# A fused RWKV6 attention and expert block: other order of work in the first steps, in step six, and of one weight addition

## The chip, the core and the metric

The kernel runs on one core of one Trainium2 chip. Such a core has five engines, each with its own queue of instructions that runs in order: TensorE (PE in the profile, its weight loads PEld), VectorE (DVE), ScalarE (ACT), GpSimd (POOL) and SyncE (SP), which here only issues transfers. ScalarE issues some transfers too. The metric is the time of one execution on the device in microseconds (us); lower is better. The kernel before takes 573.67 us, the median of three runs from 573.4 to 574.68.

## The reference

```python
def _attn_ref(r, k, v, w, u):                 # batch 4, heads 8, seq 768, head_dim 48
    state = np.zeros((B, H, D, D)); y = np.zeros_like(r)
    for t in range(S):
        kt, vt, rt, wt = (k[:, :, t], v[:, :, t], r[:, :, t], w[:, :, t])
        cur = np.einsum('bhd,bhe->bhde', u[None] * kt, vt)
        y[:, :, t] = np.einsum('bhd,bhde->bhe', rt, state + cur)
        state = wt[:, :, :, None] * state + np.einsum('bhd,bhe->bhde', kt, vt)
    return y

def _moe_ref(x, w_in, w_out):                 # 3072 tokens, d_model 384, d_ff 2048
    h = x @ w_in
    sp = np.maximum(h, 0.0) + np.log1p(np.exp(-np.abs(h)))
    return (h * erf(sp)) @ w_out              # x is y with the heads side by side
```

The first part is a recurrence over time, with a decay w that differs for each channel and time; u is a bonus for the token itself. The second is a two-layer block over all tokens with the activation h * erf(softplus(h)). The weights w_in and w_out are given in float64 and have to be made into float32 on the chip.

## The kernel before, in words

**Steps.** The work is cut into 12 steps (s = 0 to 11): six stretches of 128 tokens for each of two halves of the batch. In a step each 128 tokens are two chunks of 64 (HC). Inside a chunk the recurrence is done by levels: at level n, pairs of neighbouring blocks of 2^(n-1) tokens meet, r of the right block with k of the left block. `level_products` (line 691) is the matmul of one level into a PSUM bank `pp`; `scale` (lines 357 in step zero and 364 elsewhere) is VectorE's product that multiplies the halves of r and k in place by the decay over the level's blocks; `take_level` (lines 701, VectorE with a mask, and 708, ScalarE, for level 6) puts the products in their place in the matrix `own`. The next level's matmuls need the scale, and the scale overwrites what this level's matmuls read. The decays over blocks, the totals, are made by GpSimd (`plan_totals`, line 386, for steps 0 and 1; `prepare`, line 438, for the others). For level 1 a copy `rk1` is made, in which one half is multiplied by u (`multiply_u`, lines 408 to 419).

Then `from_own` (line 723) multiplies `own` with v into the PSUM tile `y`, `state_part` (line 798) makes the new part of the state from v and the transposed k (`kT`), `middle` is the state between the two chunks, `through_state` (line 749) adds what comes from the state to `y`. ScalarE copies `y` into `xT`; a part of it, `y3`, goes to other rows, by transfers (line 784), or in step zero by a matmul, the `hop` (line 764). `fence` (line 732) is a small VectorE copy that reads `y`.

**The second block.** `hidden` (line 1206) is x @ w_in for a step, eight pieces of 12 passes, each emptied by ScalarE (line 1215). `project` (line 1238) is the second matmul for step 0, and `project_fast` (line 1328) for the later ones, a scheme with seven products instead of eight which needs sums of weights (`mix_weights`, line 1266) and of the gated values (`blend`, lines 1305 to 1311). They are put between the parts of later steps' attention.

**The weights.** `convert` turns 16 blocks (0 to 7 of w_in, 8 to 15 of w_out) into float32. For each block there is a load by SP ("l", lines 271 to 275, let go by a one-element copy that waits for something on purpose), two ScalarE operations ("b", line 289 or 291, and "r", line 297), one or two of VectorE ("h", lines 306 and 311) and an add on GpSimd ("o", line 319). "j" is "h" and "o" together. The strings of CONVERT say which of them are sent at which level of steps 1 to 3.

**The order.** It is written out by hand: the program is under a manual schedule, so each engine runs its instructions in the order in which Python issues them. A generator made by `prepare` for the next step (`following`) is advanced by `next(following)` at chosen places. Step 0 is `attend_first`, steps 1 to 4 `attend`, steps 5 to 11 `attend_late`. In the last, strings such as "s P" say what is put where: s is a softplus on ScalarE, P a piece of `project_fast`, H one of `hidden`, F a turn of `following`. DIRECT is 4; steps 7 to 11 are "joined", steps 5 and 6 are not.

**The start.** `load_first` issues SP's loads of r, k, u, w and the masks; `stay_warm` (line 1034) issues matmuls on the identity that nothing reads, six before the first useful products and two twice among the level-1 products of step 0; `keep_busy` (line 1043) issues a matmul on zeros into a bank that is not yet used. `wait_for` (line 942) is a one-element GpSimd copy that waits for a scale.

## Time and profile before

| | before |
|---|---|
| median of three runs | 573.67 us (573.4 to 574.68) |
| the profiled execution | 573.88 us, span 572.1 us |
| PE busy | 563.8 us, 99% of the span |
| VectorE busy | 452.4 us, 79% |
| ScalarE busy | 359.2 us, 63% |
| GpSimd busy | 244.6 us, 43% |
| transfers | 63.24 MB, mean 111 GB/s |

A row of the timeline has the start in us from the beginning of the span, the duration, the engine, the line of the kernel, the operation, the tile that is written and what is read, and in brackets how long the engine was idle before it and what ended that. Matmuls in float32 appear as two passes each, so "x12" is six matmuls. The ends of matmuls are modelled, so PE looks busy across short gaps; the starts show them. A row of the chain of waits has start, duration, engine, tile and line.

### The profile page before, as it was taken

How to read it: one execution, taken by the hardware profiler on the slowest of the kernel's cores; microseconds unless marked ns; L12 is line 12 of the kernel's file. 1: busy time of each engine (PE TensorE's matmuls, PEld its weight loads, DVE VectorE, ACT ScalarE, POOL GpSimd, SP SyncE). 2: the span in 40 equal slices, each digit the busy share in tenths (PEclk: the TensorE clock that was granted, in tenths of full speed). 3: DMA queues.
4: the chain of work that ended last, by engine and by line, in shares of the span. 5: the costliest groups of instructions: out<-in, count | busy, mean ns of one | idle time of the engine just before them, and what ended most of it. 6: DMA issues, size and time to landing. Idle time of an engine off the chain costs nothing.

```text
span 572.1 us, 16713 instructions
## 1 busy us (share of the span) xinstructions
PE 563.8 (99%) x7320; PEld 501.2 (88%) x7320; DVE 452.4 (79%) x509; ACT 359.2 (63%) x495; POOL 244.6 (43%) x262
## 2 busy tenths in 40 slices
PE   8999999999999999999999999999999999999997
PEld 6688887578998998998998898899899899989997
DVE  7776886999899999699789689689778587477730
ACT  3658877646368867756765766666775771489500
POOL 3567380832884884283575176077073000000000
DMA  8596671440426215245235236335232301000000
GB/s 264 192 315 252 218 230 58 172 158 10 148 69 183 82 63 181 42 147 173 41 123 199 39 111 203 48 112 166 47 111 85 47 9 35 3 2 1 28 29 28
DMA packets 54081, 63.24 MB, mean 111 GB/s; under 512 B 35160, under 2 KB 40568, under 8 KB 52984
## 3 DMA queue, kind: packets, MB, share of 16 engines
q1 hardware_dynamic: 53624, 61.98, 34.4%
q8 instruction: 57, 0.93, 0.7%
q10 hardware_dynamic: 384, 0.20, 0.1%
q14 instruction: 16, 0.13, 0.1%
HBM read 52.39 MB, written 8.69 MB: 107 GB/s over the span
## 4 chain that ended last, share of the span: by engine, by line
PE 75%; DVE 5%; POOL 2%; ACT 1%; issue 1%; ACTq 0%; POOLq 0%
PE m L1328 33%; PE m L1206 27%; PE c L1431 6%; PE pp L691 2%; PE y L723 2%; PE y L749 1%; DVE in L364 1%; PE pp L798 1%; POOL tot_sb L438 1%; POOL w_out_sb L319 1%; PE m L1238 1%; DVE h L1171 1%; PE c L1328 0%; ACTq L784 0%; PE pp L1116 0%
## 5 line engine op out<-in xcount | busy, mean ns | idle before, releaser
L1206 PE MATMUL m<-xT,w_in_sb 128*128 128x256 f32 x960 | 214.5, 381 | 0.2 <-ACT h L1215 0.2
L1206 PEld LDWEIGHTS m<-xT,w_in_sb 128*128 128x128 f32 x960 | 180.1, 190 | 25.2 <-ACT h L1215 0.6
L364 DVE TENSOR_TENSOR in<-in,tot_sb 128x1024 f32<-128x1024 f32 (+1 forms) x55 | 75.7, 1375 | 6.3 <-PE pp L691 5.0
L1215 ACT COPY h<-m 128x512 f32<-128x512 f32 x80 | 46.2, 580 | 51.6 <-PE m L1206 51.3
L1328 PE MATMUL m<-mixed,h 128*128 128x192 f32 x320 | 56.7, 331 | 0.0
L1328 PE MATMUL m<-w_out_sb,h 128*128 128x192 f32 x320 | 56.1, 329 | 0.0
L1328 PEld LDWEIGHTS m<-mixed,h 128*128 128x128 f32 x320 | 51.8, 190 | 0.8
L1328 PEld LDWEIGHTS m<-w_out_sb,h 128*128 128x128 f32 x320 | 52.0, 190 | 0.5
L1328 PE MATMUL m<-w_out_sb,room 128*128 128x192 f32 x288 | 49.7, 326 | 0.0
L1328 PEld LDWEIGHTS m<-w_out_sb,room 128*128 128x128 f32 x288 | 47.3, 190 | 0.1
L493 POOL TENSOR_TENSOR words<-words,own 128x384 f32<-128x384 f32 x21 | 31.2, 1488 | 26.4 <-DVE words L524 13.0
L1166 ACT ACT_TABLE_LOAD x28 | 35.9, 1283 | 8.7 <-DVE h L1171 6.7
L691 PEld LDWEIGHTS pp<-in 48*48 48x48 f32 (+4 forms) x2368 | 30.1, 120 | 11.2 <-issue 5.4
L534 POOL TENSOR_TENSOR words<-words 128x384 f32<-128x384 f32 x28 | 38.7, 1410 | 0.0
L486 POOL TENSOR_TENSOR own<-rest 128x384 f32<-128x384 f32 x7 | 8.5, 1210 | 69.2 <-ACT o L1334 69.2
L1162 ACT ACT_TABLE_LOAD x28 | 35.9, 1283 | 1.8 <-issue 1.3
L691 PE MATMUL pp<-in 48*48 48x32 f32 (+4 forms) x2368 | 33.9, 206 | 0.6 <-DVE in L364 0.6
L438 POOL TENSOR_TENSOR tot_sb<-tot_sb 128x256 f32<-128x256 f32 (+4 forms) x50 | 30.8, 616 | 3.8
L559 DVE TENSOR_REDUCE sums<-rk 128x16 f32<-128x768 f32 (+2 forms) x31 | 31.3, 1022 | 0.0
L1162 ACT ACTIVATE room<-h 128x1024 f32<-128x1024 f32 x28 | 29.6, 1057 | 0.3
L534 POOL TENSOR_TENSOR rk<-words 128x384 f32<-128x384 f32 x28 | 29.6, 1088 | 0.0
L319 POOL TENSOR_TENSOR w_out_sb<-w_out_sb,rest 128x768 int32<-128x768 int32 x8 | 18.7, 2340 | 21.6 <-DVE w_out_sb L311 21.6
(215 smaller groups left out, 1013.2 us busy)
## 6 DMA issues: line engine op xcount, KB each, us to landing
in<-in_rkw SPq DMA_DIRECT2D x8, 1024.0 KB, 5.2
words<-in_moe_w_in SPq DMA_DIRECT2D x16, 384.0 KB, 5.4
words<-in_moe_w_out SPq DMA_DIRECT2D x16, 384.0 KB, 5.9
words<-in_rk_rows SPq DMA_DIRECT2D x8, 768.0 KB, 5.4
w<-in_rkw SPq DMA_DIRECT2D x11, 512.0 KB, 6.8
v<-in_v SPq DMA_DIRECT2D x12, 384.0 KB, 5.7
out<-o SPq DMA_DIRECT2D x23, 192.0 KB, 3.6
in<-in_rkw SPq DMA_DIRECT2D x7, 512.0 KB, 5.8
```

Of the source, the lines that this page charges most:

```text
L364: nc.vector.tensor_mul(halves, halves, view(tots[level - 1], 0, [[1, n], [2, nb], [0, half]]))
L438: nc.gpsimd.tensor_mul(new, pair[:, :, 0], pair[:, :, 1])
L493: engine.tensor_mul(to, to, of[:, :, None, :].to_broadcast([P, NEAR // 2 // half, half, D]))
L534: engine.tensor_mul(to[:, i], r[:, half:], k[:, part * rows + i, None].to_broadcast([P, half, D]),)
L559: nc.vector.tensor_reduce(out=to, in_=of, axis=mybir.AxisListType.X, op=ALU.add)
L691: nc.tensor.matmul(to, lhsT=rk(1, n)[rows(e), s0 : s0 + m], rhs=right, start=True, stop=True,)
L1162: nc.scalar.activation(sp_room, chunks[0], AF.Softplus)
L1166: nc.scalar.activation(at, sp_room, AF.Erf)
L1206: nc.tensor.matmul(ps[:, ff, :], lhsT=w_in_sb[:, g * FG + f + ff, kk * P : (kk + 1) * P], rhs=xT[:, kk, :], start=kk == 0, stop=kk == KT - 1,)
L1215: nc.scalar.copy(h[:, f : f + FT, :], ps[:])
L1328: nc.tensor.matmul(to, lhsT=a[:, f], rhs=b[:, f], start=start and f == 0, stop=f == FG - 1, skip_group_check=True,)
L1431: nc.tensor.matmul(to[:, f], lhsT=turns["weights"][b][:, i * FT + f], rhs=turns["tokens"][a], start=a + b in STARTS and not f, stop=True, ...
```

## The change

It has these parts, and nothing else of the program differs.

- The load of u is issued by ScalarE, ahead of its first table load, and no longer by SP between the first two loads of r and k.
- Seven warming products are issued at the start, not six.
- In step 0, level 5 (MASKED) is put in its place by four ScalarE copies of 16 rows (`take_blocks`), not by VectorE's masked copy.
- The copy `rk1` of step 1: the half for r stays on ScalarE at the same place; the half for k is made by GpSimd (two products and a copy) behind step 0's last `wait_for`.
- The load of weight block 1 is let go by the total of level 5 on GpSimd, at level 4, and no longer by `own` at level 2; the load of w for step 1 stays behind it on SP. The load of block 2 is let go by a ScalarE copy behind `middle`, not by a GpSimd copy behind `fence`.
- The eight transposes of k in step 0 go to one bank, without the `keep_busy` before them; VectorE copies the first half, ScalarE the second. One of the two conversions "h" of block 0 comes ahead of `fence`. "b" of block 1 and its "r" and "h" come behind `through_state`.
- In step 1, "h" of a block comes behind `scale` at every level, and at level 1 behind the product that writes `own`.
- In step 3, the first turn of `following` is left out at level 2 and made up at level 3. With this the addition "o" of the weight block that is sent at level 3 is issued ahead of step 4's totals on GpSimd and no longer behind them.
- In step 6 alone, the first project piece P comes behind `from_own`, `through_state` and the load of the next step.

```diff
@@ -193,8 +193,8 @@
         turns["first"] = t5 = t[:].rearrange("p x n t -> p (x n t)").rearrange(
             "p (j x n t) -> p j x n t", j=NJ, x=2, n=NP
         )
+        nc.scalar.dma_start(out=u_sb[:], in_=u)
         nc.sync.dma_start(out=t5[:, 0], in_=rkw[0][:, 0:2, b0])
-        nc.sync.dma_start(out=u_sb[:], in_=u)
         nc.sync.dma_start(out=t5[:, 1, 0], in_=rkw[0][:, 0, b1])
         nc.sync.dma_start(out=t5[:, 1, 1], in_=rkw[0][:, 1, b1])
         nc.sync.dma_start(out=ws[0][:, b0], in_=rkw[0][:, 2, b0])
@@ -411,6 +411,15 @@
                     )
                     nc.vector.tensor_copy(out=plain[0], in_=plain[1])
                     return
+                if s == 1 and x:
+                    for j in range(NJ):
+                        of = slice(j * NP, (j + 1) * NP)
+                        nc.gpsimd.tensor_mul(
+                            with_u[0][:, of], with_u[1][:, of],
+                            u_sb[:, :, None].to_broadcast([P, NP, C // 2]),
+                        )
+                    nc.gpsimd.tensor_copy(out=plain[0], in_=plain[1])
+                    return
                 for p in range(NP):
                     of = slice(p, None, NP)
                     nc.scalar.mul(
@@ -422,6 +431,7 @@
                 for i in range(parts):
                     for x in range(2):
                         multiply_u(i, x)
+                        yield
                 return
             yield
             yield
@@ -711,6 +721,18 @@
 
 
 
+    def take_blocks(own, pp, level):
+
+        half = 1 << (level - 1)
+        got = pp[:].rearrange("p e n t -> p (e n) t")
+        for s0 in range(0, C, HC):
+            for b in range(HC // 2 // half):
+                of = slice(s0 + 2 * b * half, s0 + (2 * b + 1) * half)
+                t = (2 * b + 1) * half
+                nc.scalar.copy(
+                    own[of, :, t : t + half], got[of, :, b * half : (b + 1) * half]
+                )
+
     def from_own(s, own, swap):
         vt = loaded[s][1]
         for j in range(NJ):
@@ -872,12 +894,15 @@
         level_products(pp, RK, LOG - 1)
         scale(s, LOG - 1)
         take_level(own, pp, LOG - 1)
-        run("front", None)
+        behind = before and not joined
+        run_late(s, "s" if behind else "s P")
         if before:
             from_own(before, ready[before][0], 0)
             through_state(before, xTs[before])
             if s + 1 < n_steps:
                 load_step(s + 1)
+        if behind:
+            run_late(s, "P")
         if joined:
             ps = state_products()
             next(following, None)
@@ -956,7 +981,7 @@
                 scale(0, level, batch=j)
             turns["pp"] = products([P, NE, JP, HC])
             keep_busy(turns["pp"], (DM,))
-            take_level(own, pp, level)
+            (take_blocks if level == MASKED else take_level)(own, pp, level)
             wait_for(1 << level - 1)
             if level == 2:
                 totals(2, part=slice(batch // 2, batch))
@@ -966,10 +991,11 @@
                 stages["b"](0, 0)
                 stages["b"](0, 1)
                 stages["r"](0)
-                for _ in prepare(1):
-                    pass
+                second = prepare(1)
+                next(second)
                 nc.sync.dma_start(out=vt[:], in_=v[0])
-                stages["l"](1, own[:, 0, 2:3])
+            if level == LOG - 2:
+                stages["l"](1, ready[0][1][LOG - 1][:, 0:1])
                 nc.sync.dma_start(out=ws[1][:], in_=rkw[1][:, 2])
         totals = plan_totals(1)
         pp = turns.pop("pp")
@@ -977,46 +1003,42 @@
             level_products(pp, first_pair, LOG, half)
             scale(0, LOG, batch=j)
         take_level(own, pp, LOG)
+        wait_for(HC - 1)
+        next(second)
 
         kT = att.tile([P, NH, D], FP32, name="kT", bufs=1)
         kT_by_e = kT[:].rearrange("p (e n) d -> p e n d", e=NE)
-        turned = [products([P, NE, JP, HC])]
-        keep_busy(turned[0], (DM,))
-        for j, half in enumerate(halves):
-            if j:
-                turned.append(products([P, NE, JP, HC]))
-            for i, n in enumerate(half):
-                nc.tensor.transpose(
-                    turned[j][:, 0, 2 * i : 2 * i + 2], first_pair(1, n), ident[:]
-                )
+        turned = products([P, JP, P])
+        turns["next"] = 1 - turns["next"]
+        for n in range(JP):
+            nc.tensor.transpose(turned[:, n, :], first_pair(1, n), ident[:])
         from_own(0, own, 1)
-        for half, ps, copy in zip(halves, turned, (nc.scalar.copy, nc.vector.tensor_copy)):
+        for half, copy in zip(halves, (nc.vector.tensor_copy, nc.scalar.copy)):
             copy(
                 kT_by_e[:, :, half.start : half.stop],
-                ps[:, 0].rearrange("p (n e) d -> p e n d", e=NE)[..., :D],
+                turned[:, half.start : half.stop].rearrange("p n (e d) -> p e n d", e=NE)[..., :D],
             )
-        stages["b"](1, 0)
-        stages["b"](1, 1)
+        stages["h"](0)
         fence()
-        stages["l"](2, seen[:, 0:1])
-        load_v(1)
-        stages["h"](0)
         stages["h"](0)
         ps = [[products([P, NE, JP, HC], 1 - e)[:, e] for e in range(NE)]]
         state_part(0, kT, ps, (0,))
         from_own(0, own, 0)
         nc.scalar.copy(middle[rows(1)], ps[0][1][rows(1), :, :D])
         nc.vector.tensor_copy(middle[rows(0)], ps[0][0][rows(0), :, :D])
+        stages["l"](2, middle[:, 0, 0:1], True)
+        load_v(1)
+        stages["o"](0)
+        nc.gpsimd.tensor_mul(faded[1][:], middle[:], ends[:, :, 1:2].to_broadcast([P, JP, D]))
+        through_state(0, xT)
+        stages["b"](1, 0)
+        stages["b"](1, 1)
         stages["r"](1)
         stages["h"](1)
         stages["h"](1)
-        wait_for(HC - 1)
-        stages["o"](0)
-        nc.gpsimd.tensor_mul(faded[1][:], middle[:], ends[:, :, 1:2].to_broadcast([P, JP, D]))
         totals(1)
         stages["o"](1)
         totals(*range(2, LOG + 1))
-        through_state(0, xT)
 
         def pending():
             part = products([P, NE, JP, HC], turns["next"])[:, 0]
@@ -1069,12 +1091,10 @@
                 level_products(pp, rk, level)
             if level == LOG and s == DIRECT:
                 spread_blocks(s + 1, pp)
-            if s == 1 and 2 < level:
-                stages["h"](level + 1)
             scale(s, level)
             if s == 1 and level == 2:
                 turns.pop("pending")()
-            if s == 1 and level < 3:
+            if s == 1 and level > 1:
                 stages["h"](level + 1)
             if s == 1 and level > 1:
                 nc.gpsimd.tensor_copy(out=block_sb[:, 0:1], in_=K[:, 0, 0:1])
@@ -1089,8 +1109,12 @@
                 )
             else:
                 take_level(own, pp, level)
+            if s == level == 1:
+                stages["h"](2)
             later_on = (s, level) in ((1, 4), (DIRECT, LOG))
-            if level > 1 and not later_on:
+            if level > 1 and not later_on and (s, level) != (DIRECT - 1, 2):
+                next(following, None)
+            if (s, level) == (DIRECT - 1, 3):
                 next(following, None)
             if (s, level) == (DIRECT, LOG - 1):
                 next(following, None)
@@ -1511,18 +1535,18 @@
 
 
     JOINED = set(range(DIRECT + 3, n_steps))
-    STAGES_LATE = ("front", "near", 0, 1, 2, 3, 4)
+    STAGES_LATE = ("near", 0, 1, 2, 3, 4)
     LATE = {
         DIRECT + 1: (
-            "s P", "m", "ey P m P s P ep P", "P m k22y F P k11p", "S1 F F",
+            "m", "ey P m P s P ep P", "P m k22y F P k11p", "S1 F F",
             "S2 S3 H k12y S4 H F", "s H ey m H H F s H ep H H",
         ),
         n_steps - 1: (
-            "s P", "m", "ey P w w w w w w w m s P P ep P w w w w w w w w w w w w", "m P P t t", "", "", ""
+            "m", "ey P w w w w w w w m s P P ep P w w w w w w w w w w w w", "m P P t t", "", "", ""
         ),
     }
     USUAL = (
-        "s P", "m", "ey P m s P P ep P", "m k22y P F P k11p F F", "S1", "S2 S3 H k12y S4 H F",
+        "m", "ey P m s P P ep P", "m k22y P F P k11p F F", "S1", "S2 S3 H k12y S4 H F",
         "s H ey m H H F s H ep H H",
     )
 
@@ -1595,7 +1619,7 @@
     with tc.manual_schedule(
         engines={getattr(mybir.EngineType, x) for x in ("PE", "DVE", "Activation", "Pool", "SP")}
     ):
-        stay_warm(6)
+        stay_warm(7)
         for t in (*states[0], *states[1], middle):
             nc.gpsimd.memset(t[:], 0.0)
         nc.gpsimd.memset(over_blocks[:], 1.0)
```

## The prediction

> **What bounds the kernel now.** I read the page first: its busy times, then the slices.
>
> ```profile
> span 572.1 us, 16713 instructions
> PE 563.8 (99%) x7320; PEld 501.2 (88%) x7320; DVE 452.4 (79%) x509; ACT 359.2 (63%) x495; POOL 244.6 (43%) x262
> ```
>
> TensorE (PE) is the bound, so only its gaps can be won, or work taken from it. PE's modelled ends hide gaps, so I went next to the timeline and looked at starts: a group should last its passes times the pace of long groups. L1206 runs x24 in 5.38 us in the chain of waits, 0.224 us a pass, so 12 passes last 2.69.
>
> ```profile
> 36.29 2.86 PE L1206 MATMUL m<-xT,w_in_sb 128*128 128x256 f32 x12
> 37.57 0.96 DVE L306 TENSOR_SCALAR w_in_sb<-y 128x768 int32<-128x768 int32 x1 [0.56 <-ACT y L289]
> 38.45 1.21 DVE L364 TENSOR_TENSOR in<-in,tot_sb 128x1024 f32<-128x1024 f32 x1
> 39.72 1.03 PE L691 MATMUL pp<-in 48*56 48x32 f32 x64 [0.57 <-DVE in L364]
> ```
>
> 36.29 + 2.69 = 38.98, and L691 starts at 39.72: a gap of 0.73. VectorE (DVE) did a weight conversion (L306) ahead of the scale (L364) that PE needed. The same stands at 43.15, 0.17 us. The chain of waits then shows the largest gap:
>
> ```profile
> 103.53 1.82 POOL w_out_sb L319
> 105.36 1.99 POOL tot_sb L438
> ...
> 111.43 2.48 POOL w_out_sb L319
> 113.95 4.14 PE m L1238 x12
> ```
>
> GpSimd (POOL) does six products of step four (L438, to 111.3) before it adds the last block of output weights. PE had done four passes from 111.30; at the pace of L1238 (x16 from 92.22 to 97.57, 0.33 each) they end at 112.64, so it stands 1.3 us. Behind 114 us PE's starts show nothing above 0.5 us. Ahead of 28 us PE follows a chain through VectorE and ScalarE (ACT), read from the timeline:
>
> ```profile
> 7.09 0.92 PE L691 MATMUL pp<-rk 48*64 48x64 f32 x32
> 9.00 0.69 PE L691 MATMUL pp<-rk 48*64 48x64 f32 x32
> 18.88 0.70 DVE L701 COPY_PREDICATED own<-mask_sb,pp 128x512 f32<-128x512 int32 x1
> 22.88 1.00 ACT L289 ACTIVATE m<-words 128x384 f32<-128x384 f32 x2 [1.38 <-DVE w_in_sb L306]
> 23.90 0.47 ACT L1008 COPY middle<-pp 48x384 f32<-48x384 f32 x1
> 25.23 1.82 POOL L1015 TENSOR_TENSOR faded<-middle,tot_sb 128x384 f32<-128x384 f32 x1
> 27.39 0.92 ACT L770 COPY xT<-y 128x256 f32<-128x256 f32 x3 [1.65 <-PE y L764]
> ```
>
> xT at 27.4 to 28.3 opens the hidden products, and from there PE is nearly full. So the sum is: how much earlier L1206 first starts (27.92), plus gaps closed behind it.
>
> **The first step, part by part.**
> The 7th warming product is two passes more. The twelve there now and the start of L691 take 1.68 to 7.09, 0.45 a pass; the next warming group (x4, 7.94 to 9.00) 0.27. Ends: 0.43 (two passes of 0.22) and 0.90. The first level-1 half, 0.92, then runs at the 0.69 of the second half, which gives 0.23 back. I take +0.5, as the faster pace shows only inside the group at 7.09. VectorE's own<-pp at 9.84 and its scale at 11.47 both waited for PE, so it is on the path. That the page's clock reads 1.00 here says nothing on this. [...]
> The u load goes from SP's queue to ScalarE's ahead of its table load, and SP's next six loads are issued one slot (0.47) earlier. First VectorE work waited 0.24 for u (5.14); PE's warm-up ends later anyway: 0, with ends -0.24 and +0.3 (a late landing).
> Level 5 leaves VectorE: the 0.70 row goes, and the last two scales (19.48) can start when PE's level-6 products allow, 19.02: -0.45. ScalarE does it in four copies of 256 elements, 0.31 apart (L770 has x3 in 0.92), 1.3 us; it has room, because the second L416 group and L419 (16.19 to 18.07) go to GpSimd. They end about 19.6, ahead of the transposes (20.38), which now wait for them since they use that bank. Last scale: 20.76 + 0.5 - 0.45 = 20.8, transposes end 21.35 as before. The removed filler product (L1043 at 19.63) lies beside this: 0.
> kT copies: VectorE's half can go before the transposes are all done, so L798 starts at about 22.15 instead of 22.35. ScalarE's copy of middle (23.90) stood behind L289; now it is first, at about 23.1, so L749 ends near 24.35, not 25.08, and y3 is copied at 24.5, not 25.37. Then L289 x2 and L297 (0.94) stand between y3 and xT: 24.9 + 1.0 + 0.94 = 26.85, while PE's hop L764 ends at 26.2. xT starts at 26.9 instead of 27.39: **-0.5**. Ends: 0 (second weight block late, see below) and -0.9 (the hop alone).
> That second block is asked for at 19.2 instead of 14.57, behind GpSimd's total; its load and w behind it move with it on SP's queue. Blocks on this queue landed 3.2 us (first half) and up to 5.1 us (second half) after issue around 23 us, so it lands by 24.7, just ahead of L289's second half near 25.4. The third block's gate moves from 22.44 to about 23.7, behind middle: it lands near 29, and L289 for it, at 28.45 now, goes to 29.3. Its conversion ends about 31.2, when PE has just ended level 2. It is needed at 36: 0.
> GpSimd gets two 128x256 products (L386 has 0.61) and a copy of 512. The trace has no such copy; below lies 0.61, above 2.03 (L438 with two inputs beside VectorE); I take 0.9, nearer the undisturbed 1.03 of L386's 128x512. 21.1 + 1.2 + 0.9 = 23.3, and PE needs this at 24.35. GpSimd's next rows (L319 1.82, L1015, L386) begin at 23.4 against 23.45: 0. Queued behind are the totals that VectorE's scale at 32.35 waits for, and the gate of the sixth block.
>
> **Step two.** VectorE's scales go ahead of conversions, so the gaps 0.73 and 0.17 close. But ScalarE empties PE's banks behind conversions that wait for loads (waits of 3.73, 0.59 and 1.66 for words at 33.89, 36.65, 40.49), and these shift only with xT, by 0.5. Following both queues, L1206 groups start near 39.4, 43.1, 46.6 and, with ScalarE's level-6 copies just late, 51.0 instead of 52.17: 1.15 in all, so **-0.65** here. Ends 0 and -0.9.
>
> **The third output add (step four).** Moved ahead of the six products, the last block can be added from 108.4, when VectorE ends L311, to 110.9 at the 2.48 of now, 1.7 before PE needs it: **-1.3**. The totals end near 117; VectorE first reads them at 129.47. VectorE gains only 1.15 here while PE gains 2.45; its scale L364 at 141.97 to 143.19 feeds PE at 144.74, so of 1.55 slack 1.3 are used: 0, at worst +0.4.
>
> **Step six.** One project piece (2.8 us) moves behind the state products. It covered VectorE's fence, which runs at 234.35 for 0.17 just behind L723; level-5 products (0.70) still cover it. Work on PE is unchanged. ScalarE's y3 and xT, and SP's transfers behind, come 2.6 earlier, where nothing waits: 0; had the fence its 2.01 idle time against it, +2.
>
> **Sum.** -0.5 - 0.65 - 1.3 = -2.45. The profiled execution took 573.88 (span 572.1 and 1.8 around it), 0.21 above the median: 571.4 against it, 571.2 against the median 573.67.
>
> **The rivals.**
> 1. The front gives nothing: warming at 0.9, or the second block late, and the step-two gaps are refilled by loads. Only the add is left: 573.67 - 1.3 = 572.4. For it: the load waits above; against: the 0.5 has two independent sources (middle, level 5).
> 2. VectorE becomes the bound from 98 to 142, where it is busy 19.4 and 19.9 of 20 us: PE's gap reappears at 144.7, and 1.15 plus a little stays: 572.4. Against: 1.55 of slack there.
> 3. Slower: GpSimd's three new instructions. The same 128x384 product took 1.82 at 25.23, beside VectorE's two-input scale, and 0.83 at 56.57. [...] At that ratio, 2.2, the 2.1 us become 4.6, PE gets the products at 25.8, 1.45 late, and the queue behind delays the sixth block's gate by 2.4: about 573.2, no change. Strided reads with a spread operand are in no row; from three times and more (ending after 28 us) PE's level-1 group loses over 3.6 us, more than all gains: 574.9.
> 4. The moves are hidden entirely (something else, a load, holds PE at 114): 573.5. Nothing in the trace shows such a load.
>
> **How the numbers follow.** Forecast 0.60, its own range 570.3 to 572.2; rivals one and two 0.12 each; no change (three at 2.2, and four) 0.09; slower 0.07. A measurement of this kernel tells about 0.2% (1.15 us) from no change, so faster means under 572.52: the forecast and three quarters of rivals one and two, 0.78; same 0.15; slower 0.07. Range: 570.2 (all lower ends in part: -0.9, -0.9, -1.3 and small gaps) to 573.2.
>
> **What would show it.** First L1206 near 27.4; no gap above 0.3 us at 39 and 43; L1238's last group without a gap, L319 before L438 there; L691's first group near 7.6 to 7.9; new GpSimd products ended before 24.3; PE's total after 114 us unchanged. I am wrong if xT waits for the second weight block, if VectorE's releases reappear ahead of L691 in steps three and four, or if a piece of step six waits for the fence.

## The result

The changed kernel took 575.92 us (median of nine runs, 574.15 to 577.38) beside 573.45 for the kernel before on the same chip: ratio 1.0046, 95% interval 1.0031 to 1.0061, so slower by 2.5 us. In two further measurements it was 1.0076 (1.0049 to 1.0102) and 1.0046 (1.0027 to 1.0065). The forecast was 571.2 with a range to 573.2; it was wrong in sign.

The page of the changed kernel, first the span, then busy times, then TensorE's granted clock in 40 slices:

```profile
span 573.4 us, 16722 instructions
PE 563.4 (98%) x7320; PEld 501.6 (87%) x7320; DVE 455.6 (79%) x508; ACT 359.2 (63%) x495; POOL 247.3 (43%) x264
...
PEclk9998999999999999999999999999999999999999
```

TensorE's (PE's) busy time is what it was, so the loss is waiting. The fourth slice, 43 to 57 us, has a lower clock. In this execution the front did what was forecast and more. The rows of the timeline that answer to those of before:

```profile
6.51 0.69 PE L701 MATMUL pp<-rk 48*64 48x64 f32 x32
19.98 1.19 POOL L417 TENSOR_TENSOR rk<-in,u_sb 128x256 f32<-128x256 f32 x2
21.11 0.65 POOL L421 COPY rk<-in 128x512 f32<-128x512 f32 x1
23.23 0.67 PE L771 MATMUL y<-in,middle 48*48 48x64 f32 x32 [0.28 <-DVE middle L1028]
25.98 0.92 ACT L792 COPY xT<-y 128x256 f32<-128x256 f32 x3
26.49 2.86 PE L1230 MATMUL m<-xT,w_in_sb 128*128 128x256 f32 x12
```

The first hidden product (L1230, L1206 before) starts at 26.49 instead of 27.92. Of these 1.43 us, 0.58 are there already at the first level-1 product, which starts at 6.51 instead of 7.09 although one warming product more stands ahead of it; in the two other profiles of the changed kernel (experiments 9 and 5) the first hidden product starts at 26.94 and 27.93. So part of this gain is chance. GpSimd's (POOL's) new products end at 21.8, long before PE needs them. Then, at the end of step two's levels:

```profile
46.25 2.86 PE L1230 MATMUL m<-xT,w_in_sb 128*128 128x256 f32 x12
46.41 0.93 ACT L289 ACTIVATE y<-words 128x768 f32<-128x768 f32 x1
47.27 2.82 DVE L364 TENSOR_TENSOR in<-in,tot_sb 128x1024 f32<-128x1024 f32 x1 [0.25 <-POOL block_sb L1100]
48.56 1.17 ACT L718 COPY own<-pp 32x512 f32<-32x512 f32 x2
50.01 0.94 DVE L306 TENSOR_SCALAR w_in_sb<-y 128x768 int32<-128x768 int32 x1
51.05 0.66 PE L745 MATMUL y<-own,v 64*48 64x64 f32 x32 [1.95 <-ACT h L1239]
51.65 1.25 PE L1140 MATMUL pp<-ident,in 128*128 128x128 f32 x8
52.69 4.32 PE L1230 MATMUL m<-xT,w_in_sb 128*128 128x256 f32 x12
```

By the pace of 12 passes the products from 46.25 end near 48.9, and PE's starts show 2.11 us of waiting ahead of L745. The profile names ScalarE's copy of h (L1239, ended at 50.34) as the releaser, but what ended last before 51.0 is L306 on VectorE, the conversion "h" of block 7, called the shift from here on. It reads the bank `y`, into which ScalarE's L289 put block 7 at 46.41; L745 has to write `y`. In the kernel before, this shift ran ahead of the level-6 scale (L364), which took as long:

```profile
47.38 0.96 DVE L306 TENSOR_SCALAR w_in_sb<-y 128x768 int32<-128x768 int32 x1
47.86 2.86 PE L1206 MATMUL m<-xT,w_in_sb 128*128 128x256 f32 x12
48.35 2.81 DVE L364 TENSOR_TENSOR in<-in,tot_sb 128x1024 f32<-128x1024 f32 x1
50.65 0.66 PE L723 MATMUL y<-own,v 64*48 64x64 f32 x32
```

There the products of `own` (L723, L745 after the change) start 2.79 us behind the hidden ones; in the changed kernel it is 4.80. The 12 passes from 52.69 take 4.32 us, in place of 2.69. The table of stretches, whose columns are the length, busy time of each engine, granted clock, DMA share and GB/s:

```profile
49.04:52.45 3.41, 1.46 (x40) 1.35 (x40) 1.91 (x2) 1.25 (x3) 3.18 (x6) 1.00 0.47 184
52.45:55.86 3.41, 3.41 (x11) 2.78 (x10) 0.00 (x0) 2.91 (x7) 0.77 (x1) 0.50 0.02 5
```

For 3.413 us behind the wait the granted clock is 0.50, at a cost of about 1.7 us (half of 3.413, an estimate).

### The profile page after: what moved, and what is told of

It reads as the page before. It is cut to its first block, busy times and chain, and to the rows that moved or that the text cites. A ratio compares the mean times of both kernels' runs of the same rounds, so it can differ in the third digit from the quotient of the medians.

```text
span 573.4 us, 16722 instructions
## 1 busy us (share of the span) xinstructions
PE 563.4 (98%) x7320; PEld 501.6 (87%) x7320; DVE 455.6 (79%) x508; ACT 359.2 (63%) x495; POOL 247.3 (43%) x264
## 4 chain that ended last, share of the span: by engine, by line
PE 83%; DVE 9%; issue 3%; POOL 2%; ACT 2%; DMA 1%; DVEq 0%; POOLq 0%; ACTq 0%
PE m L1352 33%; PE m L1230 29%; PE c L1455 6%; PE pp L701 5%; DVE in L364 2%; PE y L745 2%; PE m L1262 2%; PE y L771 2%; PE pp L820 2%; DMA in<-in_rkw 1%; PE pp L1065 1%; DVE own L711 1%; POOL w_out_sb L1293 1%; DVE h L1195 1%; PE pp L1140 1%
## 5 line engine op out<-in xcount | busy, mean ns | idle before, releaser
L1230 PE MATMUL m<-xT,w_in_sb 128*128 128x256 f32 x960 | 215.9, 383 | 0.2 <-ACT h L1239 0.2
L1230 PEld LDWEIGHTS m<-xT,w_in_sb 128*128 128x128 f32 x960 | 181.4, 191 | 25.5 <-ACT h L1239 0.6
L364 DVE TENSOR_TENSOR in<-in,tot_sb 128x1024 f32<-128x1024 f32 (+1 forms) x55 | 79.5, 1445 | 7.0 <-PE pp L701 4.9
L1239 ACT COPY h<-m 128x512 f32<-128x512 f32 x80 | 46.2, 579 | 50.3 <-PE m L1230 50.0
L503 POOL TENSOR_TENSOR words<-words,own 128x384 f32<-128x384 f32 x21 | 30.4, 1447 | 26.4 <-DVE words L534 13.0
L448 POOL TENSOR_TENSOR tot_sb<-tot_sb 128x256 f32<-128x256 f32 (+4 forms) x50 | 31.7, 635 | 3.8
L319 POOL TENSOR_TENSOR w_out_sb<-w_out_sb,rest 128x768 int32<-128x768 int32 x8 | 18.0, 2248 | 24.5 <-DVE w_out_sb L311 24.5
```

The costliest lines, as they stand in the source:

```text
L364: nc.vector.tensor_mul(halves, halves, view(tots[level - 1], 0, [[1, n], [2, nb], [0, half]]))
L448: nc.gpsimd.tensor_mul(new, pair[:, :, 0], pair[:, :, 1])
L503: engine.tensor_mul(to, to, of[:, :, None, :].to_broadcast([P, NEAR // 2 // half, half, D]))
L1230: nc.tensor.matmul(ps[:, ff, :], lhsT=w_in_sb[:, g * FG + f + ff, kk * P : (kk + 1) * P], rhs=xT[:, kk, :], start=kk == 0, stop=kk == KT - 1,)
L1239: nc.scalar.copy(h[:, f : f + FT, :], ps[:])
```

## The experiments

All ratios are to the kernel before on the same chip, with 95% intervals.

**1. One level back.** In the changed kernel, the shift at level 6 alone goes ahead of its scale again.

```diff
+            if s == 1 and level == LOG:
+                stages["h"](level + 1)
             scale(s, level)
...
-            if s == 1 and level > 1:
+            if s == 1 and 1 < level < LOG:
                 stages["h"](level + 1)
```

> The changed kernel with one order put back: in step two, at level 6 only, the conversion's shift h(7) (L306) runs on VectorE ahead of the scale, as in the kernel before. Theory A (the bank y): TensorE's stall of 2.11 us at 48.73 comes because h(7) reads y and stands behind a scale of 2.82 us, while the products of own (L745) must write y. Then the shift ends near 48.3, and L745 starts when ScalarE's level-6 copies end, near 49.75, instead of 51.02: the stall falls to about 1.0 us, and if TensorE's clock is then not halved for 3.4 us, its cost of 1.7 us goes too. Time: 575.9 - 1.3 - 1.7 = 572.9; 574.6 if the clock still falls. Theory B (something else holds L745: ScalarE's late copies or a load): stall stays at 2 us, 575.9.

1.0023 (1.0011 to 1.0035), 573.64 against 572.51; the clock is 1.000 in all twelve runs. In its profile PE waits 0.5 us among L745's passes, not 2.1 ahead of them. A's mechanism holds; the gain is 1.3 to 3 us, by which measurement of the changed kernel it is set against.

**2. All shifts from level 3 on back ahead of their scales**, in the changed kernel.

```diff
+            if s == 1 and 2 < level:
+                stages["h"](level + 1)
             scale(s, level)
...
-            if s == 1 and level > 1:
+            if s == 1 and level == 2:
                 stages["h"](level + 1)
```

> The changed kernel with all shifts of step two from level 3 on put back ahead of their scales. Theory A (y is held by the late shift): the small stalls return (0.73 and 0.17 in the kernel before), TensorE arrives at L745 near 49.2 and starts it near 49.75, a stall of some 0.5 us, no halved clock: 575.9 - 1.3 - 1.7 = 572.9, about as with one level put back. Theory B: stall stays, 575.9 or more.

1.0010 (0.9998 to 1.0023), 572.64; no stall ahead of L745. So the order of shifts and scales makes the better part of the loss.

**3. The reverse: the kernel before with only this order.**

```diff
-            if s == 1 and 2 < level:
-                stages["h"](level + 1)
             scale(s, level)
...
-            if s == 1 and level < 3:
+            if s == 1 and level > 1:
                 stages["h"](level + 1)
...
+            if s == level == 1:
+                stages["h"](2)
```

> The kernel before with only step two's order from the change: shifts behind the scales, h(2) behind own's product. Theory A: the gaps of 0.73 and 0.17 close, but a stall of about 2 us appears ahead of L723 (L745 in the changed kernel), which then starts near 52.4 instead of 50.65: 573.45 + 1.75 = 575.2, and 576.9 if the clock is halved behind the stall. Theory B (the stall comes from the front: work that starts 1.4 us earlier meets loads that don't): the gaps close, no stall: 573.45 - 0.5 = 572.95.

1.0054 (1.0033 to 1.0074), 575.93: with the old front, too, this order loses, 3.1 us by the ratio. Its timeline:

```profile
49.38 2.86 PE L1206 MATMUL m<-xT,w_in_sb 128*128 128x256 f32 x12
50.36 2.82 DVE L364 TENSOR_TENSOR in<-in,tot_sb 128x1024 f32<-128x1024 f32 x1 [0.25 <-POOL block_sb L1078]
53.11 0.94 DVE L306 TENSOR_SCALAR w_in_sb<-y 128x768 int32<-128x768 int32 x1
54.15 0.67 PE L723 MATMUL y<-own,v 64*48 64x64 f32 x32 [1.92 <-ACT h L1215]
```

The same scale of 2.82, the same shift behind it, the same stall (2.09 by the starts). Theory B is out. Not all of the 3.1 us need be the order's: PE has two more gaps in this profile, 0.78 us ahead of 23.08 and 1.80 ahead of 29.19, for which the profile shows nothing that it waited for. The clock is at 0.997 in one run of six.

**4. Is it the bank?** The changed order is kept, and only block 7's high half goes through another bank.

```diff
+            elif i == 7:
+                base = banks[1 - turns["next"]][:].rearrange("p (e x) -> p e x", e=2)[:, :, :DM]
             else:
                 base = y[:].rearrange("p e q j t -> p e (q j t)")[:, :, :DM]
```

> The changed kernel with only the conversion of block 7 put through another bank: its high half (L289) goes into the bank of level 5, free since 47.0 us, instead of y; the order of all engines stays, so its shift still stands behind the scale of 2.8 us. Theory A (y is what holds the products of own): they no longer wait for the shift and start when ScalarE's level-6 copies end, 1.0 us behind the hidden products instead of 2.1; the transposes, which use the bank of level 5, then wait some 0.5 us for the shift, so they start 0.6 us earlier than in the changed kernel, and the wait is cut in two short ones, so that the clock is not halved (1.7 us in most runs): ratio 1.006 - 0.001 - 0.002 = 1.003. Theory B (something else holds them): one stall of 2.1 us as before, 1.006.

1.0030 (1.0015 to 1.0046), as forecast by A, and the clock is 0.999 or more in all twelve runs. Its timeline (two lines were added, so L747 is L745, L366 the scale, L308 the shift):

```profile
49.28 2.86 PE L1232 MATMUL m<-xT,w_in_sb 128*128 128x256 f32 x12
50.29 2.83 DVE L366 TENSOR_TENSOR in<-in,tot_sb 128x1024 f32<-128x1024 f32 x1 [0.26 <-POOL block_sb L1102]
52.18 1.17 ACT L720 COPY own<-pp 32x512 f32<-32x512 f32 x2
52.80 0.32 PE L747 MATMUL y<-own,v 64*48 64x64 f32 x4 [0.67 <-ACT own L720]
53.04 0.95 DVE L308 TENSOR_SCALAR w_in_sb<-pp 128x768 int32<-128x768 int32 x1
53.40 0.65 PE L747 MATMUL y<-own,v 64*48 64x64 f32 x28 [0.28 <-ACT own L720]
```

L747 now starts before the shift does, on ScalarE's copies (L720). Order and lateness of the shift are unchanged, so `y` is what held L745. What is left, 0.83 and about 0.5 us, belongs to ScalarE's level-6 copies, which the working of the prediction had called "just late".

**5. What the halved clock costs.** Four products of the identity, 8 passes, into the bank that the transposes fill anew, ahead of L745.

```diff
+        ps = products([P, JP, P])
+        if s == 1:
+            for _ in range(4):
+                nc.tensor.matmul(
+                    ps[:, :NC], lhsT=ident[:], rhs=ident[:, None, :].to_broadcast([P, NC, P]),
+                    start=True, stop=True, skip_group_check=True,
+                )
         from_own(s, own, 1)
-        ps = products([P, JP, P])
```

> The changed kernel with four products of ident (8 passes, 1.7 us) put on TensorE ahead of the products of own in step two, into the bank that the transposes behind fill anew; the wait itself stays. Theory A: the halved clock behind the wait follows from the idle time: with it filled, the granted clock is 1.00 from 50 to 60 us and the time falls by the 1.7 us that the halved clock cost, in the share of the runs that had it (six of nine): 575.1 - 1.2 = 573.9, ratio 1.0025. Theory E (the halved clock comes from elsewhere, or the chunk behind is not on the path): 575.1, ratio 1.0046.

1.0063 (1.0042 to 1.0084), 575.43: no gain, though the clock was under 0.999 in one run of twelve only. In its profile PE stood 1.64 us at 64.0, where a transfer of xT landed late. Since that could have been chance, it was run again beside the changed kernel:

> The changed kernel beside the three others, for comparison on one chip: 1.0046 and 1.0076 so far, so 1.006; stalls of 2.1, 0.6 and 0.5 us again; the clock at 0.997 in most runs.

> The kernel of filled_wait once more, beside the changed kernel. Theory A (the halved clock costs 1.7 us in the runs that have it): it is 1 to 1.5 us under the changed kernel of this call. Theory E (what the clock gives is lost at the next wait, as at 64 us in the profile of filled_wait, where TensorE stood 1.64 us for the transfer of xT): no difference, and a stall near 64 us again.

575.06 with the fill, 1.0033 (1.0022 to 1.0044), and 575.75 without, 1.0046 (1.0027 to 1.0065), on one chip; the clock was at 0.997 in three of seven runs without the fill and in none of twelve with it, and the profile of filled_again has no stall over 0.2 us at 64 us. 0.7 us is about 3/7 of 1.7, as A has it, but the intervals overlap. The changed kernel's own runs show the price better: in its three measurements those at 0.997 take 1.7, 3.0 and 0.9 us longer on average than the others. That the idle time brings the halved clock is shown by the counts: over all three measurements of the changed kernel 14 of 22 runs have 0.997, of the two filled ones 1 of 24. The wait doesn't always bring it: shifts_behind_in_before has the same wait, and 0.997 in one run of six.

**6. The third output add alone.**

```diff
-            if level > 1 and not later_on:
+            if level > 1 and not later_on and (s, level) != (DIRECT - 1, 2):
+                next(following, None)
+            if (s, level) == (DIRECT - 1, 3):
                 next(following, None)
```

> The kernel before with only the third output add moved ahead of step four's six products. Theory A: the gap of 1.3 us ahead of L1238 at 112.6 goes, and new stalls of about 0.6 us (at 124) and 0.5 us (at 145) come, since VectorE is full there: 573.45 - 0.2 = 573.2. Theory B (the new stalls come from the changed front and step two, not from this move): 573.45 - 1.3 = 572.15.

1.0017 (1.0001 to 1.0034), 573.72 against 572.51: not a gain but a small loss, barely clear of noise. And the kernel before, profiled once more:

> The kernel before once more. Theory A: the stalls of 0.73 us (38.8) and 1.26 us (112.4) that the forecast counted on were accidents of the one execution that was profiled: they are not there, GpSimd's six products of step four take 1.05 + 2.94 us as in the profile of step_six_alone, not 2.02 + 4.01. Theory H (they belong to the order): both are there.

One of the two stalls is gone. Its timeline, GpSimd's six products of step four (L438) ahead of the add (L319):

```profile
105.15 1.04 POOL L438 TENSOR_TENSOR tot_sb<-w 128x512 f32<-128x512 f32 x1
105.59 1.68 DVE L364 TENSOR_TENSOR in<-in,tot_sb 128x1024 f32<-128x1024 f32 x1 [1.11 <-PE pp L691]
106.27 2.94 POOL L438 TENSOR_TENSOR tot_sb<-tot_sb 128x256 f32<-128x256 f32 x5
109.28 1.81 POOL L319 TENSOR_TENSOR w_out_sb<-w_out_sb,rest 128x768 int32<-128x768 int32 x1
...
111.43 0.95 DVE L567 TENSOR_TENSOR rk<-words,u_row 128x768 f32<-128x768 f32 x1
111.77 5.43 PE L1238 MATMUL m<-w_out_sb,h 128*128 128x384 f32 x16
112.30 0.54 DVE L515 TENSOR_TENSOR rk<-words 128x384 f32<-128x384 f32 x1
```

The add ends at 111.1, before PE begins its last group at 111.77, and that group runs without a gap. In the execution that the prediction was made from, VectorE's scale began at 105.12, ahead of GpSimd's product at 105.32: the scale took 1.33 and the product 2.02. Here the product was first and took 1.04, and the scale took 1.68. The stall of 1.26 us stands in that one profile, and in none of the eight others with the old place of the add. Which of the two starts first doesn't explain it by itself. In shifts_behind_in_before the scale was first too (1.36, and 2.03 for the product), in front_with_h2 both started together (1.23 and 2.12), and neither has the stall. What only the execution with the stall has is a fifth product of 1.90 us, at 108.97 (0.24 to 0.52 in the eight others), and an add of 2.51 us (1.81 to 2.12). Its rows from GpSimd:

```profile
107.42 4.01 POOL L438 TENSOR_TENSOR tot_sb<-tot_sb 128x256 f32<-128x256 f32 x5
111.39 2.51 POOL L319 TENSOR_TENSOR w_out_sb<-w_out_sb,rest 128x768 int32<-128x768 int32 x1
```

Both lie beside VectorE's L567 (at 109.32 and 111.28); why they were lengthened only here stays open. The new place has a cost of its own:

```profile
107.92 1.82 POOL L319 TENSOR_TENSOR w_out_sb<-w_out_sb,rest 128x768 int32<-128x768 int32 x1 [3.09 <-DVE w_out_sb L311]
109.69 1.36 POOL L438 TENSOR_TENSOR tot_sb<-w 128x512 f32<-128x512 f32 x1
110.08 1.79 DVE L567 TENSOR_TENSOR rk<-words,u_row 128x768 f32<-128x768 f32 x1
111.13 3.93 POOL L438 TENSOR_TENSOR tot_sb<-tot_sb 128x256 f32<-128x256 f32 x5
111.79 0.96 DVE L515 TENSOR_TENSOR rk<-words 128x384 f32<-128x384 f32 x1
...
122.98 0.76 PE L691 MATMUL pp<-in 48*32 48x32 f32 x64 [0.49 <-DVE in L364]
```

This is third_add_alone. The six products now run beside VectorE's L567 and L515, which take 1.79 and 0.96 instead of 0.95 and 0.54, in a stretch where VectorE is nearly full (busy for 16.90 of the 17 us from 108 to 125); PE then waits 0.65 us near 123 and 0.50 near 143. All nine profiles with the moved add have both waits (0.61 to 0.65 and 0.49 to 0.52). From the eighth hidden piece of step two to the end these profiles take 515.5 us on average (leaving out filled_wait with its late transfer), and those with the old place 514.65 (leaving out the one with the stall): the move costs 0.85 us. The two groups don't overlap: 515.1 to 515.9 and 514.2 to 514.9.

**7. The front alone**, with step two, the add and six warming products as before: the change's parts in `load_first`, `multiply_u`, `prepare`, `take_blocks` and `attend_first`, of which the core is

```diff
-            take_level(own, pp, level)
+            (take_blocks if level == MASKED else take_level)(own, pp, level)
...
-        stages["l"](2, seen[:, 0:1])
...
+        stages["l"](2, middle[:, 0, 0:1], True)
```

> The kernel before with only the first step's changes (u load on ScalarE's queue, level 5 on ScalarE, the new places of kT, middle, the second and third weight blocks, GpSimd's products for step two); six warming products, step two, the third add and step six as before. Theory A: L1206 starts 1.4 us earlier (26.5 instead of 27.9, as in the profile of the changed kernel) and nothing takes it back: 572.5 - 1.4 = 571.1, ratio 0.9975. Theory C: the gain is lost to loads that don't start earlier (stalls ahead of L691 or L1206 between 27 and 40 us): 572.5.

1.0005 (0.9987 to 1.0023), 573.67 against 572.41 by the medians: no gain, and the clock is under 0.999 in five of twelve runs. The reason, in its timeline:

```profile
29.42 0.87 ACT L289 ACTIVATE y<-words 128x768 f32<-128x768 f32 x1 [2.24 <-DMA words<-in_moe_w_in]
30.32 0.96 DVE L306 TENSOR_SCALAR w_in_sb<-y 128x768 int32<-128x768 int32 x1 [2.28 <-ACT y L289]
31.20 1.21 DVE L1106 TENSOR_TENSOR own<-pp,first 128x1024 f32<-128x1024 f32 x1
32.46 1.52 PE L820 MATMUL pp<-v,kT 64*48 64x48 f32 x32 [1.86 <-DVE own L1106]
```

The third weight block lands later, as the prediction had it. Its shift, h(2), stands ahead of own's level-1 product in the old order and holds PE for 2.07 us. The change moves h(2) behind that product; that one part of step two's order is needed by the front:

```diff
-            if s == 1 and level < 3:
+            if s == 1 and level == 2:
                 stages["h"](level + 1)
...
+            if s == level == 1:
+                stages["h"](2)
```

> The kernel before with the first step's changes and, of step two's, only h(2) behind own's level-1 product. Theory A: front_alone lost its gain because the third weight block lands later (its conversion L289 at 29.42), so that h(2) held own's product and TensorE stood 2.07 us at 30.39, with a halved clock behind it; with h(2) behind the product no stall is left there, and L1206 starts 20.0 us behind the first level-1 product instead of 20.75: 572.4 - 0.75 = 571.65, ratio 0.9987, clocks of all runs at 0.999 or more. Theory C (the loads take the gain anyway): 572.4 or more, with stalls at 26 to 40 us.

0.9982 (0.9962 to 1.0002), 572.07, clock 0.999 or more in all twelve runs. The interval still takes in 1. From the first level-1 product to the first hidden one it is 20.0 us in its profile, against 20.6 to 21.0 in five profiles with the old front (leaving out shifts_behind_in_before with its two gaps there). Of all twelve profiles with the new front, eight have 20.0 to 20.2. The other four have 20.7 to 21.0, and in each of them PE has a gap of 0.46 to 0.59 us in this stretch, for which the profile shows nothing that it waited for.

Two pieces later the gain is not to be seen: from the first level-1 product to the third hidden piece it is 28.4 to 30.4 us (29.4 on average) in eleven profiles with the new front, without front_alone, and 29.0 to 29.4 (29.2) in the five with the old one. PE comes earlier, and the fourth weight block doesn't: ScalarE's L289 for it starts 25.5 to 28.0 us behind the first level-1 product with the new front and 25.7 to 27.1 with the old. ScalarE's copy of h, which PE waits for, stands behind it. The profile of front_h2_six (experiment 10) has the longest such wait:

```profile
34.82 0.88 ACT L289 ACTIVATE y<-words 128x768 f32<-128x768 f32 x1 [2.81 <-DMA words<-in_moe_w_in]
36.40 0.57 ACT L1239 COPY h<-m 128x512 f32<-128x512 f32 x1
37.12 3.23 PE L1230 MATMUL m<-xT,w_in_sb 128*128 128x256 f32 x7 [1.69 <-ACT h L1239]
```

Behind this wait, too, the clock was halved for 3.413 us: from 37 to 41 us its mean is 0.57.

**8. The seventh warming product, and step six,** each alone in the kernel before. First

```diff
-        stay_warm(6)
+        stay_warm(7)
```

> The kernel before with a seventh warming product and nothing else. Theory A: it delays the first level-1 product by 0.4 us on average (6.5 to 7.1 us with six and 6.5 to 7.8 us with seven in the profiles so far), 572.8, ratio 1.0007. Theory F (an earlier full clock gives it back): 572.4 or less.

0.9992 (0.9974 to 1.0010). The first level-1 product starts at 6.5 to 7.1 us in the eight profiles with six products and at 6.5 to 7.8 in the ten with seven, 0.4 later on average (the forecast had 7.6 to 7.9); the time can't tell it. What F has of a full clock was not shown: in the first profile of before the granted clock reads 1.00 from the first product on. Then step six, with the strings of LATE and USUAL as in the change:

```diff
-        run("front", None)
+        behind = before and not joined
+        run_late(s, "s" if behind else "s P")
...
+        if behind:
+            run_late(s, "P")
```

> The kernel before with only step six's three places. Theory A (forecast): nothing on the path moves, 572.5, ratio 1.000, no stall near 236 us. Theory D: the later project piece leaves TensorE waiting for VectorE's fence: up to +2 us, 574.5.

0.9999 (0.9979 to 1.0019), and no stall near 236 us.

**9. The changed kernel once more,** without an edit, as was before_again.

> The changed kernel once more, on this chip. Theory A: the stall of about 2 us ahead of L745 at 48 to 52 us and those of 0.6 (near 124) and 0.5 us (near 145) stand in this execution too, since they follow from the order; where the front starts and whether the clock halves may differ: 575.1, ratio 1.0046. Theory G (these stalls were accidents of one execution): at least one of the three is gone.

1.0076. The stalls are 2.11 us at 49.53, 0.63 at 124.0 and 0.51 at 145.3 (each place is the start of the last pass ahead of it); they belong to the order.

**10. Two tries at a better kernel.** The first is the changed kernel with experiment 1, ScalarE's L297 of block 7 behind its level-6 copies, and the add in its old place. The second of these is

```diff
-        (("", "br"),) * 2 + (("", "brl"),) * 3 + (("", "l"), ("", ""), ("", ""), ("", "brl")),
+        (("", "br"),) * 2 + (("", "brl"),) * 2 + (("", "bl"), ("", "l"), ("", ""), ("", ""), ("", "brl")),
...
+            if s == 1 and level == LOG:
+                send("r")
+                nc.gpsimd.tensor_copy(out=block_sb[:, 0:1], in_=K[:, 0, 0:1])
+                stages["o"](level + 1)
```

> The changed kernel with three things put otherwise: at level 6 of step two the shift h(7) ahead of the scale; ScalarE's low half of block 7 (L297) behind its level-6 copies, so that these end near 48.9 instead of 49.73; the third output add back in its old place. Theory A: TensorE waits at most 0.4 us ahead of the products of own, the front's 1.4 us and the closed gaps of step two stay, the stall of 1.3 us at 112 is back and those of 0.6 and 0.5 us at 124 and 145 are gone: 572.5 - 1.4 - 0.5 = 570.6, ratio 0.9967. Theory C (loads that don't start earlier take the front's gain back): 572 to 572.5.

1.0003 (0.9986 to 1.0021), where 0.9967 was forecast: a stall of about 0.5 us moves to the transposes, which read what the later scale writes. That is not the whole miss; the rest stays open. The second kernel is front_with_h2 with the edit of step_six_alone:

> The kernel before with the first step's changes, h(2) behind own's product and step six's places: all of the change but the other shifts, the third add and the seventh warming product. Theory A: as front_with_h2 (0.9982), step six adds nothing: 0.9982, some 1 us faster than before. Theory C (the 0.9982 was chance): 1.000.

0.9985 (0.9972 to 0.9998), 572.14 against 572.54. This is faster than both kernels: by some 0.9 us under the kernel before by the ratio, 0.4 by the medians, and the interval only just leaves out 1. It is the front and step six without the other shifts, the moved add and the seventh product.

## Why the prediction was wrong

1. **The failing step is "Step two", −0.65.** It priced whom a scale keeps waiting, and not whom a shift keeps waiting. Moved behind the scale, the shift holds `y`, and the next writer of `y` on PE is `from_own`. At levels 2 to 5 nobody asks for `y` before ScalarE's next block; at level 6 PE does. The prediction said of no shift what it reads and who needs that free. From the sixth hidden piece to the one behind step two's transposes it is 6.33 to 6.44 us in the three profiles of the changed kernel and 4.31 or 4.32 in the five with the old order and the old front, so the stall costs 2.0 us. Up to the sixth piece it is 19.8 to 20.1 us against 19.3 to 20.8: the gaps that were to be closed give nothing that can be seen. Over the whole stretch, from the first hidden piece to the one behind the transposes, the changed kernel takes 26.1 to 26.4 us, and the five others 23.6 to 25.1. The step thus cost 1 to 2.8 us instead of giving 0.65. The gap of 0.73 us that it was to close is no fixed price either: at that place it is 0.73 and 1.32 in the two profiles of before, and absent in those of third_add_alone and step_six_alone.
2. **What followed had no term at all:** the clock at 0.50 for 3.4 us, an estimated 1.7 us, in 14 of 22 runs (a mean clock of 0.997).
3. **The third add, −1.3, fails by itself.** The stall was real in that execution, but it is in none of the eight other profiles with the same order, so it was no price of the order. GpSimd's first and fifth product (2.02 and 1.90 us) and its add (2.51) took longer there, beside operations of VectorE; why all three only there stays open. The rival that VectorE becomes the bound was the right one, though not by the slack it was worked out from: VectorE's own operations took longer beside the moved products (L567 1.79 us instead of 0.95). VectorE's releases ahead of L691, which the prediction had named as a sign against it, came. −1.3 became +0.85.
4. **The front, −0.5, was right as far as the first hidden piece.** It gains about 0.7 us up to there in eight of twelve profiles, 0.5 on the average of all, without the warming product, for which the forecast had −1.0. Behind that the fourth block's load takes it back in most profiles, which is what rival one had of loads; the times of front_with_h2 and front_h2_six put the gain at some 0.9 to 1 us, with intervals that reach 1 or nearly do. GpSimd's new products took 1.84 us at the place of the forecast's 2.1; the rival that they would be late did not come. That the third block lands near 29 was right (L289 for it starts at 27.6 to 31.2 us in the twelve profiles); that its shift would hold own's product in the old order was not seen, and the change had met it.
5. **Step six, 0**, and the u load, 0: nothing measured speaks against these.

Worked out from the terms: front −0.7, seventh product +0.4, step two +1 to +2.8, clock +1.1 (1.7 times 14/22), add +0.85, which makes +2.65 to +4.45; measured +2.6 to +4.4 (the ratios 1.0046 and 1.0076). With −0.5 for the front both ends are 0.2 higher. The agreement is no proof of each term, since the terms come from a few profiles each.

## What to carry to other kernels

When work is moved behind a long operation on its engine, list what that work reads, and ask for each buffer who is to write it next: the cost of a late reader falls on the writer, and the releaser that the profile names may be another engine that had ended earlier, as ScalarE's copy here, at 50.34 us where the shift ended at 50.95. Before a stall is priced, see whether it belongs to the order or to that execution: a stall of 1.26 us stood in one profile of nine, and one more profile of the same kernel shows it. Where a change can make TensorE wait for some 2 us, count a slow clock behind it among the risks; here 14 of 22 runs had it. When work is moved earlier, ask whether the loads that it meets move with it.

## What the runs showed that was not expected

- **Behind a wait of 2 us TensorE's granted clock was often halved.** Its mean over the run is 0.997 in 14 of the changed kernel's 22 runs, and in 1 of 24 with the wait filled. The records of the clock change on a grid of 3.413 us that lies at another place from profile to profile: at 52.45 and 55.86 us in the changed kernel's first, at 32.08 in front_alone, at 37.22 in front_h2_six. In the changed kernel's first profile the wait lay almost whole in one stretch of the grid, 49.04 to 52.45 us, with PE busy for 1.46 us of it, and the next stretch got 0.50. In changed_again the grid cuts the same wait (at 50.25, worked out from the start of its record), the two stretches have 3.08 and 1.80 us of busy time, and the clock stayed at 1.00. The busy time of a stretch alone doesn't decide: that one of 1.80 us was followed by 1.00, one of 1.72 in front_h2_six (33.81 to 37.22) and one of 1.94 in front_alone (28.67 to 32.08) by 0.50, in the last for two stretches. In shifts_behind_in_before PE stood 2.09 us ahead of 54.15, and the clock stayed at 1.00 from 50 to 60 us. What decides stays open.
- **VectorE's and GpSimd's operations with two inputs took longer side by side**, the one that started first less so or not at all: 1.33 and 2.02 us where VectorE's scale was first (105.12 in the first profile of before), 1.68 and 1.04 where GpSimd's product was (105.15 in before_again). Alone, a scale of that size takes 1.22 us (60.00 in the changed kernel's first profile) and a GpSimd product of that size 1.03 (27.02 in the first profile of before). At level 6 of step two, in the changed kernel's first profile, the scale takes 2.82 us beside GpSimd; the add (L319) that starts 0.08 ahead of it takes 1.82, as it does alone at 51.40. The one-input shift (L306) takes 0.94 to 0.96 us in step two of that profile, 0.94 also at 50.01, where it lies wholly beside GpSimd's four products (L448, from 48.96 for 2.36).
